# The guard in the softmax's sum, four pairs of w_out sums on VectorE, and a planner that knows GpSimd's exclusion

## The chip, the cores and the metric

The kernel runs on one core of a Trainium2 chip. The metric is the device time of one execution in microseconds, where lower is better. The core has five engines that matter here: TensorE (PE, matrix products), VectorE (DVE), ScalarE (ACT), GpSimd (POOL), and SyncE (SP), which issues the transfers.

## What is computed

Block attention feeds a feed-forward layer, all in float32. Each query sees the keys less than 16 positions away and 24 summaries of blocks of 32 keys (the maximum of the keys, the mean of the values).

```python
k_sum = k.reshape(B, H, nb, 32, D).max(axis=3)
v_sum = v.reshape(B, H, nb, 32, D).mean(axis=3)
a = np.exp(scores_all - np.max(scores_all, axis=-1, keepdims=True))
a = a / (np.sum(a, axis=-1, keepdims=True) + 1e-09)
x = np.matmul(a, np.concatenate([v, v_sum], axis=2))     # 4 batches, 8 heads, 768 x 64
h = x_as_3072_by_512 @ w_in                              # w_in 512 x 2048
out = np.square(np.maximum(h, 0.0)) @ w_out              # w_out 2048 x 512
```

## The kernel before

Every product of two float32 operands is made of three matmuls with high and low halves: a value is cast to a rounded high half, and what is left is the low half. So most results need a cast on ACT and a subtraction on DVE before PE may read them.

The program has three kinds of work on the 3072 tokens. Two *plain* units (512 tokens each) run the feed-forward layer directly: for each f of 16 blocks of d_ff, FI (line 1195) is twelve matmuls with w_in, then come Relu (RL, line 1204), square (SQ) and cast (GH, line 1206) on ACT and the subtraction GL (line 1209) on DVE, and FO (line 1219) is twelve matmuls with w_out. `rl`, which RL and SQ write and GL reads last, is a single buffer, so the RL of the next f waits for the GL of this one. Behind them, *mixed* (line 1731) and *products* (line 1514) handle the other 2048 tokens with fewer products, from sums of blocks of the weights. Those sums are made while the plain units run: `combine(p)` makes the sums for eight pairs of w_out blocks (RC: two operations of 128x512, line 1300; SC: four of 128x256, line 1315; SH, the cast, line 1318; SL, the subtraction, line 1321; then a store), and `combine_in` the half sums of w_in blocks (line 1364, 128x256; line 1379, four of 128x128; 1382 and 1385 for cast and subtraction). RC and SC of the pairs are on POOL; of the half sums, two for each of eight pairs of w_in blocks, the string HALF_SUMS_BY says pair by pair whether RC and SC are on POOL (P) or on DVE (D).

The attention is made in 48 groups of scores. For each, PE makes scores (S, line 756), DVE takes the maximum with the mask (M, line 830), ACT makes the exponentials and their sums (line 887), DVE adds 1e-9 and takes the reciprocal (R, lines 899 and 900), and the normalisation (N) is either one operation on DVE (line 906, 128x472) or four activations on ACT (line 913), as the string NORMAL_BY says. Then the square blocks are transposed (T), by PE (line 926) or by DVE with a transfer (line 955), and multiplied by the values (V, line 997).

What each engine does, and in which order, comes from a planner. The class `Plan` takes tasks (`add(name, engine, cost, emit, key, ...)`), and `order` simulates all engines in time with these costs, always starting the task with the smallest key that can start. Nothing of the order is decided on the chip: each engine works through its list, and waits where an operand is not there. Tables of numbers (VISITS for the attention's groups, COMBS and SUMS for the sums, FV_AT and others) set the keys. In the planner's model, DVE's two-input operations and POOL's exclude each other; before, this is a factor by which one stretches the other (`SLOWS`, `SLOWED`).

Of the kernel before, what the change touches and what calls it, by code (L numbers as in the profile page):

```python
# [53 lines left out]
PRODUCTS = 7  # L54
FV_AT = 60.61, 233.96
FV1_LEAD = 17.0
HALVED = 2
TURN_LATE = 0.4
COMBS = 113.9, 126.8, 141.39, 159.1, 177.9, 210.24, 223.15, 214.82
Q_LEAD = 10.72  # L60
XS_LEAD = 10
R_LEAD = 9
TR_LEAD = 16.82
VISITS = 50.65, 58.31, 70.31, 76.15, 99.76, 110.62, 136.36, 142.89, 161.01, 177.12, 203.05, 215.03, 227.83, 233.26, 248.89, 277.47, 296.02, 310.51, 324.02, 346.69, 366.69, 366.74, 394.74
X_LEAD = 5.36
SPLIT_AT = -7.62
KEPT = 105.02, 3.08
GH_LEAD = 12
# [117 lines left out]
class Plan:  # L186
# [8 lines left out]
    NARROW = ("S", "V", "VM")  # L195
    SHARED = "GL", "TA", "TB", "WJ", "WW", "SL", "SLi", "XD", "XSL", "XPL", "XW", "RCi", "SCi", "N"
# [16 lines left out]
    def order(self):  # L213
# [13 lines left out]
        events, n, pipe = [], 0, 0.0  # L227
        started, narrow, slows = [], False, 0.0
        for t in self.tasks:
            kind = t.name.rstrip("0123456789_ab")  # L230
            t.narrow = t.engine == "PE" and kind in self.NARROW
            kind = "".join(c for c in kind if not c.isdigit() and c != "_")
            t.shared = t.engine == "DVE" and kind in self.SHARED
            t.late_by = 0.25 if kind == "R" else 0.0
            t.slack = self.SLACK.get(kind, 0.0)
            t.slows = self.SLOWS.get(kind, 0.3)
            t.slowed = self.SLOWED.get(kind, 1.1) if t.engine == "POOL" else 1.0

# [15 lines left out]
        while events:  # L254
            now = events[0][0]
            while events and events[0][0] <= now + 1e-9:
                t = heapq.heappop(events)[2]
                if t is None:
                    continue
                if isinstance(t, tuple):  # L260
                    ready[t[0].engine].append(t[0])
                    continue
                for b in t.take + t.use:
                    b.left -= 1
                for x in then[t]:
                    x.wait -= 1
                    if x.wait:
                        continue
                    if x.slack:
                        n += 1  # L270
                        heapq.heappush(events, (now + x.slack, n, (x,)))
                    else:
                        ready[x.engine].append(x)
# [6 lines left out]
            for e, tasks in ready.items():  # L280
# [20 lines left out]
                started.append(t)  # L301
                cost = t.cost * t.slowed
                if e == "SP":
                    cost *= (0.40 + 0.065 * min(max(pipe - now, 0.0), 4.0)) / 0.42
                if e == "DVE" and free["POOL"] > now:
                    cost += t.late_by
                    if t.shared:
                        cost += slows * min(cost, free["POOL"] - now)
                if e == "POOL":
                    slows = t.slows  # L310
                free[e] = end = now + cost + self.SWITCH * (t.narrow and not narrow)
# [15 lines left out]
def attention_then_relu2_ffn(  # L327
# [4 lines left out]
    vS: bass.AP,  # L332
    vF: bass.AP,
    wW: bass.AP,
    out: bass.AP,
# [89 lines left out]
    MIXED_STEP = 1.54, 1.41  # L425
    X_BY = 19.41, 14.78
# [3 lines left out]
    HALF_AT = 26.97, 32.0  # L430
    MX = 0.95
# [374 lines left out]
    def softmax(g, by_pe=False):  # L806
# [15 lines left out]
        for i, t_s in enumerate(t_S[g]):  # L822
# [49 lines left out]
            def total(js=js):  # L872
                nc.vector.tensor_reduce(
                    out=nm.tile[:, NPAIR : 2 * NPAIR][:, js], in_=pr.tile[:, js, :KEYS], op=ALU.add, axis=AX.X
                )
# [9 lines left out]
        def exps(p):  # L885
            x = pr.tile[:, p, :KEYS]
            nc.scalar.activation(  # L887
                x, score_tile(g, p % parts)[:, p] if by_pe else x, AF.Exp, bias=nm.tile[:, p : p + 1],
                scale=SCALE if by_pe else -1.0, accum_out=nm.tile[:, NPAIR + p : NPAIR + p + 1],
            )  # L890
# [23 lines left out]

# [371 lines left out]
    def combine(p):  # L1286

        due = COMBS[p]
        ws = [woven[1, 2 * p + k] for k in range(2)]
        xs = [buf("t", 3, (P, 2 * DM), F32, f"c{'rs'[i]}{p}") for i in range(2)]  # L1290

        def block(c, w):
# [58 lines left out]
    def combine_in(p, k, due):  # L1351
# [43 lines left out]
        for i in range(2):  # L1395
# [3 lines left out]
            ))  # L1399
        t2 = add(f"SC{name}", engine, 1.7 * slow + 0.1, add_up, due + 0.8, t1, use=[x])  # L1400
        t3 = add(f"SH{name}", "ACT", 0.56, high, due + 2, [t2], use=[x])
# [459 lines left out]
    def groups(n):  # L1861

        nonlocal done_g
        while done_g < n:
# [122 lines left out]
```

## Time and profile before

| | |
|---|---|
| three runs | 582.85, 584.73, 585.45 us, median 584.73 |
| the profiled execution | 583.48 us |
| its span (first to last instruction) | 581.0 us |
| mean granted clock of TensorE | 0.996 |
| busy: PE, DVE, ACT, POOL | 563.0, 452.2, 373.7, 134.5 us |

The page gives each engine's busy time and the groups of instructions that took it. Other views tell who waited for whom, when each instruction started, and how busy each engine was in a stretch of time. Times in the timeline are counted from the first instruction.

### The profile page before, as it was taken

How to read it: one execution, taken by the hardware profiler on the slowest of the kernel's cores; microseconds unless marked ns; L12 is line 12 of the kernel's file. 1: busy time of each engine (PE TensorE's matmuls, PEld its weight loads, DVE VectorE, ACT ScalarE, POOL GpSimd, SP SyncE). 2: the span in 40 equal slices, each digit the busy share in tenths (PEclk: the TensorE clock that was granted, in tenths of full speed). 3: DMA queues.
4: the chain of work that ended last, by engine and by line, in shares of the span. 5: the costliest groups of instructions: out<-in, count | busy, mean ns of one | idle time of the engine just before them, and what ended most of it. 6: DMA issues, size and time to landing. Idle time of an engine off the chain costs nothing.

```text
span 581.0 us, 12047 instructions
## 1 busy us (share of the span) xinstructions
PE 563.0 (97%) x4052; PEld 460.2 (79%) x4052; DVE 452.2 (78%) x1015; ACT 373.7 (64%) x968; POOL 134.5 (23%) x193
## 2 busy tenths in 40 slices
PE   7879999999999899999999999999999999999997
PEld 6668787888887688887888888888888888888885
DVE  4899999685799997879976978869932656868864
ACT  1899899786757787768765768464634642454442
POOL 4300010167669469500043430000000000000000
PEclk9999999999999999999999999999999999999999
DMA  8899996989997999999988888866875566667672
GB/s 298 295 382 340 332 337 243 323 327 341 304 381 236 327 358 338 364 333 335 312 271 246 268 257 257 268 181 192 256 240 175 178 195 192 196 195 226 196 227 98
DMA packets 88082, 157.15 MB, mean 270 GB/s; under 512 B 9066, under 2 KB 30926, under 8 KB 88022
## 3 DMA queue, kind: packets, MB, share of 16 engines
q1 hardware_dynamic: 88022, 156.39, 82.2%
q8 instruction: 32, 0.52, 0.4%
q14 instruction: 28, 0.23, 0.1%
HBM read 111.30 MB, written 44.66 MB: 268 GB/s over the span
## 4 chain that ended last, share of the span: by engine, by line
PE 76%; DVE 9%; DMA 8%; SPq 3%; issue 2%; ACT 1%; DVEq 0%; ACTq 0%
PE o L1514 23%; PE o L1731 14%; PE h L1195 9%; PE o L1219 9%; PE sz L1731 8%; PE att L1514 4%; PE x L997 3%; DMA raw<-wW 3%; PE att L756 2%; PE sa L1731 2%; PE att L1731 2%; DMA v<-vS 1%; DMA fv_lent<-vS 1%; DMA out<-os 1%; DVE ci L1379 1%
## 5 line engine op out<-in xcount | busy, mean ns | idle before, releaser
L1496 ACT CAST gh<-g 128x512 fp32r<-128x512 f32 x112 | 69.3, 621 | 63.2 <-DVE gl L1501 30.5
L1514 PE MATMUL o<-gh,w 128*128 128x512 f32 x384 | 103.0, 390 | 0.0
L1501 DVE TENSOR_TENSOR gl<-g,gh 128x512 fp32r<-128x512 f32 x112 | 76.8, 693 | 22.9 <-ACT gh L1496 22.4
L1514 PEld LDWEIGHTS o<-gh,w 128*128 128x128 f32 x384 | 71.8, 188 | 15.0
L1195 PE MATMUL h<-xh,w 128*128 128x512 f32 x240 | 76.2, 399 | 3.9 <-ACT rl L1204 3.9
L1768 ACT ACTIVATE g<-g 128x512 f32<-128x512 f32 x60 | 37.6, 630 | 49.5 <-DVE g L1764 49.3
L887 ACT ACTIVATE p<-p,small 128x118 f32<-128x118 f32 x160 | 61.1, 387 | 1.6 <-DVE small L830 1.6
L1219 PE MATMUL o<-w,gh 128*128 128x512 f32 x240 | 61.9, 394 | 0.0
L1514 PE MATMUL o<-gl,w 128*128 128x512 f32 x192 | 59.2, 389 | 0.0
L1195 PEld LDWEIGHTS h<-xh,w 128*128 128x128 f32 x240 | 45.1, 191 | 14.2 <-ACT rl L1204 4.7
L1219 PEld LDWEIGHTS o<-w,gh 128*128 128x128 f32 x240 | 44.4, 188 | 9.7 <-issue 0.4
L1195 PE MATMUL h<-xl,w 128*128 128x512 f32 x120 | 47.2, 394 | 0.0
L1514 PEld LDWEIGHTS o<-gl,w 128*128 128x128 f32 x192 | 36.0, 188 | 7.6
L1731 PE MATMUL o<-w,w 128*128 128x512 f32 x160 | 40.6, 390 | 0.0
L769 POOL COPY kb<-kb 128x96 f32<-128x96 f32 x25 | 10.9, 435 | 107.1 <-PE att L756 36.4
L1774 POOL TENSOR_TENSOR g<-g 128x512 f32<-128x512 f32 x16 | 22.6, 1418 | 53.7 <-ACT g L1768 53.1
L1731 PEld LDWEIGHTS o<-w,w 128*128 128x128 f32 x160 | 30.0, 188 | 6.3
L1491 DVE TENSOR_TENSOR g<-g 128x512 f32<-128x512 f32 x48 | 33.9, 716 | 1.2 <-POOL g L1774 0.7
L830 DVE CUSTOM_DVE_ANT_0 p<-att,mask 128x118 f32<-128x118 f32 x152 | 32.5, 272 | 2.6 <-PE att L756 2.6
L1731 PE MATMUL sz<-xh,w 128*128 128x512 f32 x128 | 34.5, 391 | 0.0
L1219 PE MATMUL o<-w,gl 128*128 128x512 f32 x120 | 33.6, 389 | 0.0
L1764 DVE CUSTOM_DVE_ANT_0 g<-sz,g 128x512 f32<-128x512 f32 x32 | 21.9, 685 | 13.2 <-ACT g L1751 6.4
(201 smaller groups left out, 1186.7 us busy)
## 6 DMA issues: line engine op xcount, KB each, us to landing
raw<-wW SPq DMA_DIRECT2D x32, 512.0 KB
w<-scr_t SPq DMA_DIRECT2D x64, 256.0 KB
w<-scr_s SPq DMA_DIRECT2D x64, 256.0 KB
w<-scr_a SPq DMA_DIRECT2D x48, 256.0 KB
w<-scr_i SPq DMA_DIRECT2D x44, 256.0 KB
turn<-a SPq DMA_DIRECT2D x18, 512.0 KB
scr_t<-ci SPq DMA_DIRECT2D x16, 512.0 KB
v<-vS SPq DMA_DIRECT2D x34, 192.0 KB
```

The lines of the kernel that those rows point to most:

```text
L830: nc.vector.tensor_tensor_reduce(out=pr.tile[:, j, :KEYS], in0=score_at(g, 0, j), in1=mask_of(g)[0], scale=-SCALE, scalar=-NEG, op0=ALU.ad ...
L887: nc.scalar.activation(x, score_tile(g, p % parts)[:, p] if by_pe else x, AF.Exp, bias=nm.tile[:, p : p + 1], scale=SCALE if by_pe else -1 ...
L1195: nc.tensor.matmul(cut(h), lhsT=lhs.tile[:, k // 2, k % 2 * P : (k % 2 + 1) * P], rhs=rhs[:, k, c0 : c0 + n], start=(i == 0), stop=(i == 3 ...
L1219: nc.tensor.matmul(o_of(o, t).rearrange("p (h c) -> p h c", h=2), lhsT=terms[i][0].tile[:, (t - t0) * P : (t - t0 + 1) * P], rhs=terms[i][ ...
L1491: lambda x=x, ins=ins, op=op: nc.vector.tensor_tensor(out=x.tile, in0=ins[0].tile, in1=ins[1].tile, op=op),
L1496: f"GH{s}_{n}", "ACT", 0.54, lambda x=x, gh=gh: nc.scalar.copy(out=gh.tile, in_=x.tile), due - GH_LEAD, ready,
L1501: lambda x=x, gh=gh, gl=gl: nc.vector.tensor_tensor(out=gl.tile, in0=x.tile, in1=gh.tile.bitcast(F32), op=ALU.subtract),
L1514: nc.tensor.matmul(o.tile[:, d], lhsT=chunk.tile[:, w * HALF + d * P : w * HALF + (d + 1) * P], rhs=y.tile, start=begins and w == 0 and y ...
L1731: nc.tensor.matmul(o.tile, lhsT=lhs(w, k), rhs=y[k], start=begins and i == 0, stop=i == 5, skip_group_check=not begins,)
L1764: lambda: nc.vector._custom_dve(TENSOR_ADD_SAT, out=to.tile, in0=o.tile, in1=x.tile, s0=HUGE, s1=0.0), key, deps,
L1768: f"G{name}_{s}", "ACT", 0.63, lambda: nc.scalar.activation(to.tile, to.tile, AF.Square), key + 0.7, [t], use=[to]
L1774: f"{name}_{s}", engine, cost, lambda: tensor.tensor_tensor(out=to.tile, in0=a.tile, in1=b.tile, op=ALU.subtract), key, deps,
```

## The change

Six things change.

1. The tile `nm` (in the order's rows `small`) has 16 columns for a group in place of 12. The sums are in columns 8 to 11, and columns 12 to 15 hold 1e-9, set once by three memsets on POOL. R adds the two by one reduction over both (TENSOR_REDUCE, 128x4 from 128x8) where it had a TENSOR_SCALAR.
2. COMBS_BY sends RC and SC of the pairs 0, 1, 2 and 6 of w_out to DVE.
3. HALF_SUMS_BY moves which half sums are on DVE: pairs 4, 6, 7 before, 0 and 4 now.
4. NORMAL_BY has 10 groups on ACT, where it had 20.
5. The planner models exclusion exactly: it keeps the ends of the running POOL operation's pieces, and a DVE operation that needs the shared port waits for the piece that is running, and pushes the ones behind it.
6. The tables of keys are new numbers. `batch_means` and its input are new, too, but MEANS_BY = "PP" leaves them unused.

```diff
-NORMAL_BY = "DDDDDDDDDDDDAADDDDDAADDADDAAAADDADDDDAADAAAAAAAA"
-HALF_SUMS_BY = "PPPPDPDD"
+NORMAL_BY = "DDDDDDDDDDDDDDDAADDAADAADDADDADDADDDDDDDDDDADDDD"
+COMBS_BY = "DDDPPPDP"
+HALF_SUMS_BY = "DPPPDPPP"
...
-COMBS = 113.9, 126.8, 141.39, 159.1, 177.9, 210.24, 223.15, 214.82
+COMBS = 115.38, 133.05, 111.75, 161.18, 184.3, 225.3, 201.76, 232.08
...
-    SLOWS = dict(RC=1.0, TA=1.0, TB=1.0, RCi=0.75, SCi=0.4, SC=0.2)
-    SLOWED = dict(RCi=1.2, SCi=1.35, RC=1.12, SC=1.2, KC=1.4, TA=0.95, TB=0.95)
+    PORTED |= dict(SC=(4, 0.4), SCi=(4, 0.25))
+    PIECES = dict(RC=(1, 1.3), SC=(4, 0.74), RCi=(1, 0.74), SCi=(4, 0.46), KC=(1, 0.27), TA=(1, 1.3), TB=(1, 1.3), C=(0, 0.0))
...
+                if t.ported:
+                    at = now
+                    for _ in range(t.ported[0]):
+                        i = next((i for i, x in enumerate(pool) if x > at), None)
+                        if i is not None:
+                            cost += pool[i] - at
+                            at = pool[i]
+                            pool[i + 1 :] = [x + t.ported[1] for x in pool[i + 1 :]]
+                        at += t.ported[1]
...
-    SUMS = 121.7, 129.74, 148.43, 166.33, 195.88, 201.13, 197.53, 197.25, 153.98, 169.96, 168.64, 165.29, 173.06, 198.45, 180.64, 190.85
+    SUMS = 125.86, 118.08, 156.5, 165.84, 192.11, 199.75, 201.36, 194.59, 144.23, 176.48, 167.97, 152.24, 157.23, 194.46, 181.73, 203.98
...
+    def make_guard():
+        for x in small:
+            nc.gpsimd.memset(x[:, 3 * NPAIR :], 1e-9)
...
-        nm = buf("nm", 3, (P, 3 * NPAIR), F32, f"nm{g}")
+        nm = buf("nm", 3, (P, 4 * NPAIR), F32, f"nm{g}")
...
         def inverse():
-            den, rec = nm.tile[:, NPAIR : 2 * NPAIR], nm.tile[:, 2 * NPAIR : 3 * NPAIR]
-            nc.vector.tensor_scalar_add(rec, den, 1e-9)
+            rec = nm.tile[:, NPAIR : 2 * NPAIR]
+            nc.vector.tensor_reduce(
+                out=rec, in_=nm.tile[:, 2 * NPAIR :].rearrange("p (k n) -> p n k", k=2), op=ALU.add, axis=AX.X
+            )
             nc.vector.reciprocal(out=rec, in_=rec)
...
+        by_pool = COMBS_BY[p] == "P"
+        engine, tensor = ("POOL", nc.gpsimd) if by_pool else ("DVE", nc.vector)
...
-            nc.gpsimd.tensor_tensor(
+            tensor.tensor_tensor(
                 out=halves(k, 0), in0=ws[k][0].tile.bitcast(F32), in1=ws[k][1].tile.bitcast(F32), op=ALU.add
             )
```

Three places show how the order moves. The first is DVE's list where the second unit begins (`gl_0` is the GL of its first f; `cr` and `cs` are the tiles of a w_out pair, `p` the exponentials, `a` their transposes). Before:

```order
L1385 TENSOR_TENSOR ci_1_1906<-ci_1_1906 128x4x128
L899 TENSOR_SCALAR small_88<-small_88 128x4
L900 RECIPROCAL small_88<-small_88 128x4
L899 TENSOR_SCALAR small_72<-small_72 128x4
L900 RECIPROCAL small_72<-small_72 128x4
L906 TENSOR_TENSOR p_83<-p_83,small_72 128x4x118
L955 STREAM_TRANSPOSE a_2046<-p_82 128x4x128
L955 STREAM_TRANSPOSE a_2046<-p_83 128x4x128
L1321 TENSOR_TENSOR cr_1955<-cr_1955 128x2x256
L1321 TENSOR_TENSOR cs_1956<-cs_1956 128x2x256
L1209 TENSOR_TENSOR gl_0_2095<-rl_0_2044,gh_0_2054 128x512
```

Now (line 965 is R's reduction, 1277 is GL, 1391 is SL, 1370 is RC and 1385 SC):

```order
L968 RECIPROCAL small_72<-small_72 128x4
L974 TENSOR_TENSOR p_83<-p_83,small_72 128x4x118
L1023 STREAM_TRANSPOSE a_2046<-p_82 128x4x128
L1391 TENSOR_TENSOR cr_1957<-cr_1957 128x2x256
L1023 STREAM_TRANSPOSE a_2046<-p_83 128x4x128
L1391 TENSOR_TENSOR cs_1958<-cs_1958 128x2x256
L1370 TENSOR_TENSOR cr_2090<-w_2_916 128x2x256
L1370 TENSOR_TENSOR cs_2091<-w_849 128x2x256
L1277 TENSOR_TENSOR gl_0_2097<-rl_0_2050,gh_0_2055 128x512
L1385 TENSOR_TENSOR cs_2091<-cr_2090,cs_2091 128x256
L1385 TENSOR_TENSOR cr_2090<-cs_2091,cr_2090 128x256
L1385 TENSOR_TENSOR cr_2090<-cr_2090 128x256
```

The subtractions of the pair before stand there as they did; the two additions (line 1370) and the four others (line 1385) of a pair are new in the row, on both sides of `gl_0`.

The second place is DVE's list from the GL of the seventh f of that unit (`gl_6`) to that of the eighth (`gl_7`); `ci` are the tiles of half sums. Before:

```order
L955 STREAM_TRANSPOSE a_2609<-p_82 128x4x128
L899 TENSOR_SCALAR small_72<-small_72 128x4
L900 RECIPROCAL small_72<-small_72 128x4
L1385 TENSOR_TENSOR ci_0_2446<-ci_0_2446 128x4x128
L1385 TENSOR_TENSOR ci_1_2428<-ci_1_2428 128x4x128
L1379 TENSOR_TENSOR ci_0_2566<-ci_0_2566 128x128 x4
L955 STREAM_TRANSPOSE a_2609<-p_83 128x4x128
L1364 TENSOR_TENSOR ci_0_2657<-w_1684 128x2x128
L1364 TENSOR_TENSOR ci_0_2657<-w_1665 128x2x128
L1385 TENSOR_TENSOR ci_0_2566<-ci_0_2566 128x4x128
L1379 TENSOR_TENSOR ci_0_2657<-ci_0_2657 128x128 x4
L1209 TENSOR_TENSOR gl_7_2672<-rl_7_2614,gh_7_2659 128x512
```

Now, with the row ahead of `gl_6` (lines 1434 and 1449 make a half sum, 1455 is its subtraction):

```order
L1434 TENSOR_TENSOR ci_1_2578<-w_1137 128x2x128
L1277 TENSOR_TENSOR gl_6_2585<-rl_6_2504,gh_6_2512 128x512
L1023 STREAM_TRANSPOSE a_2602<-p_82 128x4x128
L965 TENSOR_REDUCE small_72<-small_72 128x4
L968 RECIPROCAL small_72<-small_72 128x4
L1434 TENSOR_TENSOR ci_1_2578<-w_1176 128x2x128
L974 TENSOR_TENSOR p_83<-p_83,small_72 128x4x118
L1455 TENSOR_TENSOR ci_1_2406<-ci_1_2406 128x4x128
L1023 STREAM_TRANSPOSE a_2602<-p_83 128x4x128
L1455 TENSOR_TENSOR ci_0_2501<-ci_0_2501 128x4x128
L1449 TENSOR_TENSOR ci_1_2578<-ci_1_2578 128x128 x4
L1277 TENSOR_TENSOR gl_7_2667<-rl_7_2621,gh_7_2641 128x512
```

Two times four operations of line 1379 and two of 1364 stood between these two GLs; now four and one of their counterparts stand there, and a normalisation (line 974).

The third place is PE's list around f = 6 of the first unit (`h_6` is FI, `o` are FO's, `t` a transposition). Before:

```order
L1219 MATMUL o_67<-w_828,gh_3_1015 128x512 x4
L1219 MATMUL o_66<-w_828,gh_3_1015 128x512 x4
L1219 MATMUL o_67<-w_828,gl_3_1022 128x512 x2
L1219 MATMUL o_66<-w_828,gl_3_1022 128x512 x2
L926 MATMUL t_1083<-ident,p_83 128x128 x4
L1195 MATMUL h_6_1091<-xh,w_975 128x512 x2
L1195 MATMUL h_6_1091<-xl,w_975 128x512
```

Now (line 1263 is FI, 1287 is FO, 994 the transposition):

```order
L1287 MATMUL o_67<-w_849,gl_3_1039 128x512 x2
L1287 MATMUL o_66<-w_849,gl_3_1039 128x512 x2
L994 MATMUL t_1085<-ident,p_83 128x128 x4
L1287 MATMUL o_67<-w_893,gh_4_1060 128x512 x4
L1287 MATMUL o_66<-w_893,gh_4_1060 128x512 x4
L1287 MATMUL o_67<-w_893,gl_4_1080 128x512 x2
L1287 MATMUL o_66<-w_893,gl_4_1080 128x512 x2
L1263 MATMUL h_6_1118<-xh,w_982 128x512 x2
L1263 MATMUL h_6_1118<-xl,w_982 128x512
```

FI of f = 6 stood directly behind the transposition; now FO of f = 4 stands between the two.

## Rows read from the trace of the kernel before

**Rows 1.** The page's busy shares of the engines, in us of the span.

```profile
PE 563.0 (97%) x4052; PEld 460.2 (79%) x4052; DVE 452.2 (78%) x1015; ACT 373.7 (64%) x968; POOL 134.5 (23%) x193
```

**Rows 2.** Waits on PE: line waited for, us in total, times, longest.

```profile
PE h L1195 <- ACT rl L1204: 3.9, 3, 2.7
...
PE o L1731 <- DVE g L1764: 0.3, 1, 0.3
```

**Rows 3.** Timeline of PE at two places: start, us, instruction, idle before.

```profile
69.79 0.73 PE L1195 MATMUL h<-xh,w 128*128 128x512 f32 x2 [0.81 <-ACT rl L1204]
...
72.65 1.98 PE L1219 MATMUL o<-w,gh 128*128 128x512 f32 x8
...
201.23 1.22 PE L1195 MATMUL h<-xh,w 128*128 128x512 f32 x2 [2.72 <-ACT rl L1204]
...
205.62 1.08 PE L1219 MATMUL o<-w,gh 128*128 128x512 f32 x4
```

**Rows 4.** Busy us of PE, PEld, DVE, ACT, POOL, then clock, DMA, GB/s.

```profile
100.00:146.40 46.40, 46.40 (x372) 37.98 (x371) 32.25 (x90) 35.74 (x99) 22.10 (x27) 1.00 0.92 329
146.40:202.00 55.60, 52.51 (x446) 42.55 (x445) 50.69 (x127) 39.42 (x112) 38.35 (x51) 0.99 0.90 308
201.20:204.60 3.40, 3.37 (x8) 2.69 (x9) 3.40 (x20) 3.36 (x12) 2.47 (x4) 0.51 1.07 390
```

**Rows 5.** Waits on ACT of line 1204.

```profile
ACT rl L1204 <- DVE gl L1209: 13.8, 10, 3.9
```

**Rows 6.** Timeline of ACT before the stall ends.

```profile
195.08 1.25 ACT L913 ACTIVATE p<-p,small 128x118 f32<-128x118 f32 x4 [0.38 <-DVE small L900]
...
199.92 0.62 ACT L1382 CAST ci<-ci 128x512 fp32r<-128x512 f32 x1 [1.00 <-DVE ci L1379]
...
200.58 0.60 ACT L1204 ACTIVATE rl<-h 128x512 f32<-128x512 f32 x1
```

**Rows 7.** Timeline of DVE, three of line 1209.

```profile
183.69 0.85 DVE L1209 TENSOR_TENSOR gl<-rl,gh 128x512 fp32r<-128x512 f32 x1
...
193.05 0.95 DVE L1209 TENSOR_TENSOR gl<-rl,gh 128x512 fp32r<-128x512 f32 x1
...
199.81 0.68 DVE L1209 TENSOR_TENSOR gl<-rl,gh 128x512 fp32r<-128x512 f32 x1
```

**Rows 8.** DVE's groups of half sums from 146.4 to 202 us.

```profile
L1379 DVE TENSOR_TENSOR ci<-ci 128x128 f32<-128x128 f32 x16 | 6.8, 463 | 0.2
...
L1364 DVE TENSOR_TENSOR ci<-w 128x256 f32<-128x256 f32 x8 | 5.7, 740 | 0.5 <-DMA out<-os 0.5
```

**Rows 9.** DVE's groups over the whole span, shapes apart.

```profile
L1209 DVE TENSOR_TENSOR gl<-rl,gh 128x512 fp32r<-128x512 f32 x30 | 25.2, 842 | 6.2 <-ACT gh L1206 6.2
...
L899 DVE TENSOR_SCALAR small<-small 128x4 f32<-128x4 f32 x48 | 12.2, 254 | 5.5 <-ACT p L887 4.5 <-ACT qvpa_lent L887 1.0
...
L900 DVE RECIPROCAL small<-small 128x4 f32<-128x4 f32 x48 | 8.5, 178 | 1.6
...
L906 DVE TENSOR_TENSOR qvpa_lent<-qvpa_lent,small 128x472 f32<-128x472 f32 x8 | 5.1, 641 | 0.1
...
L873 DVE TENSOR_REDUCE small<-qvpa_lent 128x2 f32<-128x236 f32 x2 | 0.8, 394 | 0.5 <-ACT qvpa_lent L870 0.5
```

**Rows 10.** POOL's groups of sums over the whole span.

```profile
L1379 POOL TENSOR_TENSOR ci<-ci 128x128 f32<-128x128 f32 x40 | 24.9, 643 | 1.2
...
L1364 POOL TENSOR_TENSOR ci<-w 128x256 f32<-128x256 f32 x20 | 16.1, 822 | 18.5 <-DMA scr_t<-ci 7.2 <-DMA scr_s<-cr 6.2 <-DVE ci L1379 5.1
...
L1300 POOL TENSOR_TENSOR cs<-w 128x512 f32<-128x512 f32 x8 | 13.0, 1622 | 17.0 <-DVE w L1145 14.8 <-PE h L1195 2.3
...
L1315 POOL TENSOR_TENSOR cs<-cr,cs 128x256 f32<-128x256 f32 x8 | 7.5, 942 | 0.4
```

**Rows 11.** One GL on DVE, and the matmuls on PE that read it.

```profile
164.85 1.13 DVE L1209 TENSOR_TENSOR gl<-rl,gh 128x512 fp32r<-128x512 f32 x1
...
178.85 1.07 PE L1219 MATMUL o<-w,gl 128*128 128x512 f32 x4
```

More of the change, by code (lines that the diff above doesn't have):

```diff
@@ L232, in order @@
             kind = "".join(c for c in kind if not c.isdigit() and c != "_")
-            t.shared = t.engine == "DVE" and kind in self.SHARED
-            t.late_by = 0.25 if kind == "R" else 0.0
+            t.ported = self.PORTED.get(kind) if t.engine == "DVE" else None
+            if t.ported and not t.ported[1]:
+                t.ported = 1, t.cost - 0.13
+            t.pieces = self.PIECES.get(kind, (1, t.cost)) if t.engine == "POOL" else None
             t.slack = self.SLACK.get(kind, 0.0)
-            t.slows = self.SLOWS.get(kind, 0.3)
-            t.slowed = self.SLOWED.get(kind, 1.1) if t.engine == "POOL" else 1.0
         def can(t):
@@ L258, in order @@
                 if t is None:
+                    continue
+                if not isinstance(t, tuple) and t.engine == "POOL" and t.end + self.HOP > now + 1e-9:
+                    n += 1
+                    heapq.heappush(events, (t.end + self.HOP, n, t))
                     continue
@@ L301, in order @@
                 started.append(t)
-                cost = t.cost * t.slowed
+                cost = t.cost
                 if e == "SP":
                     cost *= (0.40 + 0.065 * min(max(pipe - now, 0.0), 4.0)) / 0.42
[L305 to L310, printed above, removed]
+                if t.ported:
[7 more added lines that the diff above has]
+                        at += t.ported[1]
+                    port = at
+                    if pool and pool[-1] > free["POOL"]:
+                        free["POOL"] = running.end = pool[-1]
+                        n += 1
+                        heapq.heappush(events, (pool[-1], n + 0.5, None))
+                if t.pieces:
+                    k, d = t.pieces
+                    at = max(now, port) if k else now
+                    pool, running = [at + d * (i + 1) for i in range(k)], t
+                    cost = pool[-1] + 0.03 - now if k else cost
                 free[e] = end = now + cost + self.SWITCH * (t.narrow and not narrow)
@@ L594, in attention_then_relu2_ffn, with batch_means, load, sums @@
     t_means = add("means", "POOL", 1.0, make_means, -88)
+    def make_guard():
+        for x in small:
+            nc.gpsimd.memset(x[:, 3 * NPAIR :], 1e-9)
+    t_guard = add("guard", "POOL", 0.3, make_guard, -87)
+    NQT = DM // P
+    ROWS = BLOCK // 4
+    def batch_means(b):
+        key = FV_AT[b - 2]
+        xs = [buf("t", 3, (P, 2 * DM), F32, f"fv{b}_{i}") for i in range(BLOCK // ROWS)]
+        n = NB * NQT
+        def load(i):
+            nc.sync.dma_start(out=xs[i].tile[:n], in_=vB[b - 2, :, i])
+        def sums(i):
+            return xs[0].tile[:n, i * P : (i + 1) * P]
+        def add_up(i):
+            nc.vector.tensor_reduce(
+                out=sums(i), in_=xs[i].tile[:n].rearrange("p (r c) -> p c r", c=P), axis=AX.X, op=ALU.add
+            )
+        def mean():
+            k = len(xs)
+            nc.vector.tensor_reduce(
+                out=sums(k), in_=xs[0].tile[:n, : k * P].rearrange("p (k c) -> p c k", c=P), axis=AX.X, op=ALU.add
+            )
+            nc.vector.tensor_scalar_mul(out=sums(k), in0=sums(k), scalar1=1.0 / BLOCK)
+        t = None
+        for i, x in enumerate(xs):
+            tl = add(
+                f"FV{b}_{i}", "SP", 0.42, lambda i=i: load(i), key + FV_GAP * i, take=[x], size=4 * n * 2 * DM * RUN4,
+                begin=key - 2 + FV_GAP * i, keeps=True,
+            )
+            t = add(f"VR{b}_{i}", "DVE", 1.15, lambda i=i: add_up(i), key + FV_GAP * i + 3, [tl, t], use=[xs[0], x] if i else [x])
+        t = add(f"VR{b}", "DVE", 0.85, mean, key + FV_GAP * 3 + 4, [t], use=xs[:1])
+        t_VS[b] = [add(
+            f"VD{b}", "SP", 0.42, lambda: nc.sync.dma_start(out=scr_v[b].rearrange("n (q c) -> (n q) c", c=P), in_=sums(len(xs))),
+            t.key + 1.5, [t], use=xs[:1], size=4 * NB * DM,
+        )]
     def batch_v(b):
@@ L873, in total @@
                 nc.vector.tensor_reduce(
-                    out=nm.tile[:, NPAIR : 2 * NPAIR][:, js], in_=pr.tile[:, js, :KEYS], op=ALU.add, axis=AX.X
+                    out=nm.tile[:, 2 * NPAIR : 3 * NPAIR][:, js], in_=pr.tile[:, js, :KEYS], op=ALU.add, axis=AX.X
                 )
@@ L1399, in combine_in @@
             ))
-        t2 = add(f"SC{name}", engine, 1.7 * slow + 0.1, add_up, due + 0.8, t1, use=[x])
+        t2 = add(f"SC{name}", engine, 1.8 if by_pool else 1.2, add_up, due + 0.8, t1, use=[x])
         t3 = add(f"SH{name}", "ACT", 0.56, high, due + 2, [t2], use=[x])
```

48 lines of the change are left out of this document (28 added, 20 removed).

## The prediction

> **What bounds the kernel now.** I read the page first, for the busy shares: TensorE is busy 97% of the span, VectorE 78% [rows 1]. PE does the same instructions before and after the change, so only its gaps can be won or lost, and gaps that PE makes itself (start-up apart) are few. The second view is who waited for whom on PE: after the start-up, the matmuls of line 1195 (FI, the w_in products of one f) waited three times for the Relu of line 1204, 3.9 us in all and 2.7 at the longest, and one product of the mixed stage waited 0.3 us for VectorE [rows 2]. The third is PE's timeline. The longest wait is 2.72 us ahead of 201.23, and the twelve matmuls behind it take 4.39 us to the next group's start (205.62); a like group at 69.79 to 72.65 takes 2.86 us [rows 3]. So the stall has a second cost of 4.39 - 2.86 = 1.53 us: in the 3.4 us behind it the granted clock is 0.51, which is the lower of TensorE's two levels, 1.2 GHz, where the stretch of 100 to 146.4 us shows 1.00 [rows 4]. PE was idle for 2.72 us just before. Together that one place costs 4.25 us. At 69.79 the wait is 0.81 us [rows 3], and the third must be 3.9 - 2.7 - 0.8 = 0.4 us.
>
> Why the Relu is late: on ScalarE, line 1204 waits ten times for VectorE's line 1209, 13.8 us in all [rows 5]; `rl` is a single buffer, and GL (line 1209) is its last reader. Ahead of the late Relu at 200.58 stands the cast of line 1382, which idled 1.00 us for VectorE's line 1379 [rows 6], the quarter sums of a w_in half sum. On VectorE three GLs lie at 183.69, 193.05 and 199.81, that is 9.4 and 6.8 us apart [rows 7], while PE needs about 5.7 us for each f (FI and FO, twice the 2.86). VectorE, then, is behind in this stretch: from 146.4 to 202 us it is busy 50.69 of 55.6 us (91%); from 100 to 146.4 only 32.25 of 46.4, so 14.15 us are free there, while GpSimd works 22.10 us in the first and 38.35 us in the second [rows 4].
>
> **The change, part by part.** *Half sums.* From 146.4 to 202 VectorE does 16 operations of line 1379 and 8 of 1364, four half sums, in 6.8 + 5.7 = 12.5 us [rows 8]. In the new order only two of them stand between the GLs of f 0 and 7 of the second unit; two others (pair 0) stand before the first unit's last GLs. An operation of 128x256 costs about 0.41 us (estimate: the reduction that reads 236 columns takes 0.394 [rows 9]), one of 128x128 less, some 0.27 (estimate: about two thirds of it). A half sum free of GpSimd is then 2 x 0.41 + 4 x 0.27 = 1.9 us; the measured 12.5 / 4 = 3.1 is the upper bound.
>
> *Four w_out pairs.* A pair on VectorE is two operations of 128x512 at 0.68 (the GL at 199.81 [rows 7]) and four of 128x256 at 0.41: 3.0 us, 12 us for four. On GpSimd it takes 2 x 1.62 + 4 x 0.94 = 7.0 us [rows 10]; 28 us leave that engine, two more half sums come (2 x 0.82 + 4 x 0.64 = 4.2 us each, at the means of [rows 10]). The order puts pairs 2 and 0 and the first two operations of pair 1 ahead of the second unit's first GL.
>
> *Normalisations.* Ten more are on VectorE. One is 0.64 us when GpSimd is quiet [rows 9]; ScalarE loses four activations each, which start over 1.25 us for four [rows 6]. Most lie behind 300 us, where PE shows no wait for it; two (g = 12, 13) fall around 105 us.
>
> *The guard.* 48 additions of 1e-9 to 128x4 take 0.254 us in the mean, the reciprocal of the same shape 0.178 [rows 9]. A reduction of 128x8 to 128x4 is not in the trace; from below nothing at all bounds it, from above the reduction of 2 x 118 to 2 columns, 0.394 [rows 9]. I take 0.18, as its size is nearest to the reciprocal's. That is -3.6 us of VectorE over the run, with bounds of -12 and +6.7; six of these lie in the stretch of the stall, so -0.4 us there (bounds -1.5 to +0.8). The three memsets lie in GpSimd's start-up, ahead of work that waits for scores.
>
> One rule speaks against this edit. The Trainium skill (VectorE: DVE Perf Modes, Rules for kernel authors) says that a tensor_reduce on a hot path is the slowest operation of that engine and should be restructured away. By the trace 236 columns take 0.394 us, so at eight columns the rule has little to act on; by the rule's worst reading, the 0.394, the sum would be 0.8 us worse at the stall.
>
> *The ledger of the two stretches.* From 100 to 146.4, VectorE gains 3.0 + 3.0 + 1.4 (pairs) + 3.8 (half sums) + 1.3 (normalisations) = 12.5 us, against 14.15 free: it fits with little left, and what spills is met by slack. The GL at 164.85 is read by PE only at 178.85 [rows 11], so 13 us of lateness cost nothing there. From 146.4 to 202, it loses 12.5 and gains 1.6 (the rest of pair 1) + 3.8 (two half sums): -7.1 us. The Relu of 200.58 has to come 2.72 us earlier, that of the 0.4 us stall 0.4: 7.1 covers both, unless more than 4.4 us spill over from the first stretch.
>
> *What else is saved.* GL takes 0.842 us in the mean and 0.68 when nothing is on GpSimd [rows 7, 9]: 30 x 0.16 = 4.8 us of waiting, part of which goes as GpSimd has 28 - 8.4 = 20 us less to do. I count it as reserve.
>
> *PE's order.* In the new order the group that waited 0.81 us stands behind another FO group of some 2.86 us, whose operands are older; that covers the wait. Without that cover the 0.81 comes back.
>
> *Planner.* The exact exclusion costs nothing by itself; it acts through these orders.
>
> **Sum.** -4.25 (stall and clock) - 0.8 - 0.4 = -5.45; the 0.3 us at VectorE's other wait stays. Every retimed table brings small waits somewhere: I add two of the sizes seen, 0.4 and 0.8, so -4.25 in all. The profiled execution took 583.48 us (span 581.0 and 2.48 around it): 579.2. The median of the runs shown is 584.73, 1.25 higher; by it the sum is 580.5. I say 579.5.
>
> **Rivals.** A measurement of this kernel can tell about 0.5% (2.9 us) from no change: faster is below 581.8, slower above 587.6.
>
> 1. *The backlog moves.* VectorE gains 12.5 us in a stretch with 14.15 free. If its waits for data (which made part of the free time) stay, over 10 us of GL lateness arise by the second unit's first f, and one stall of the same kind, with its clock, comes there: -5.45 + 4.25 + 1 = about 583.5. For it: the pairs stand directly ahead of GL in the row. Against: 13 us of slack and a GpSimd that is idle there, so shorter operations. 0.18.
>
> 2. *Half the relief.* 4 to 5 us spill over; the wait of 2.72 shrinks to about 1, and its clock loss falls away or not: 580.5 to 582.5. 0.12, most of it faster.
>
> 3. *Slower: GpSimd's sums come late.* ScalarE takes the casts of the sums (lines 1318, 1382) in order ahead of Relu; [rows 6] show one that idled 1.00 us. By the tables GpSimd's first sum moves from 113.9 to 152.24 us, and by the order twelve half sums of 4.2 us and pairs 3 and 4 of 7.0 us follow, 64 us of work without a break. If a sum is over 5 us behind its place, the cast stalls ScalarE, then Relu, then PE; two such places, each with its clock, cost 8.5, and if half of the 5.45 is still won, the time is 583.5 - 2.7 + 8.5 = 589.3. For it: GpSimd had 38.35 of 55.6 us of work there [rows 4]. Against: it loses the pairs. 0.10.
>
> 4. *Nothing for PE.* The reduction comes out at its upper bound and each stretch of VectorE stays as late as it was: 583.5. 0.04. The rule of the Trainium skill named above would act this way.
>
> The forecast itself, with its range of 576.5 to 581.8, has 0.56.
>
> **How the numbers follow.** Faster: 0.56 + 0.10 of the second rival = 0.66. Same: 0.18 + 0.02 + 0.04 = 0.24. Slower: 0.10. The range must leave out no more than 0.2: its low end takes in a start-up gain that I could not price, 575.5; its high end takes the first rival with the noise of the runs, 585.5, and leaves out the third.
>
> **What would show it.** Right: no PE gap over 1 us behind 60 us for line 1204's counterpart; a granted clock of 1.00 near 200 us; GLs of the second unit at most 6 us apart from f 5 to 7; the guard's reduction at about 0.18 us, not longer while GpSimd runs. Wrong: a PE gap with a half clock at 145 to 165 us (the first rival), or ScalarE waiting for GpSimd's sums at 180 to 240 us (the third), or VectorE busy over 95% in both stretches.

## The result and the profile after

The changed kernel takes 579.37 us in the median (578.37 to 581.89) against 584.73 for the kernel before in the same measurement; the ratio is 0.9912, 95% interval 0.9886 to 0.9937. The profiled execution took 579.34 us, with a span of 577.5. The prediction was 579.5.

The page gives the busy shares:

```profile
PE 563.2 (98%) x4052; PEld 460.9 (80%) x4052; DVE 456.4 (79%) x1037; ACT 365.0 (63%) x928; POOL 119.5 (21%) x184
```

PE's busy time is what it was [rows 1], so between these two executions the 3.5 us of the span are waits. VectorE's busy time does not fall: 456.4 us in place of 452.2. GpSimd loses 15 us.

Who waited for whom on PE (us in total, times, longest):

```profile
PE t L994 <- DVE qvpa_lent L974: 2.6, 2, 1.9
...
PE h L1263 <- DVE xl L1133: 1.9, 1, 1.9
...
PE h L1263 <- ACT rl L1272: 0.2, 1, 0.2
```

The wait for Relu, 3.9 us before [rows 2], is 0.2 (line 1272). A wait of 1.9 us for XL is new (line 1133, the low half of the attention's output; the tile that it reads shares two buffers with those into which FI writes, so FI waits for it). Another wait is nearly gone, at the start: at 41 us, the first matmuls of `h_0b` (FI of f = 0 for half of the first unit's tokens) waited for the cast XH, the high half of the attention's output. Before, and now:

```profile
PE h_0b L1195 <- ACT xh L1062: 1.7, 1, 1.7
```

```profile
PE h_0b L1263 <- ACT xh L1130: 0.2, 1, 0.2
```

The timeline of VectorE, at the GLs that answer to [rows 7]:

```profile
186.73 0.94 DVE L1277 TENSOR_TENSOR gl<-rl,gh 128x512 fp32r<-128x512 f32 x1
...
193.26 3.06 DVE L1449 TENSOR_TENSOR ci<-ci 128x128 f32<-128x128 f32 x4
196.25 1.23 DVE L1277 TENSOR_TENSOR gl<-rl,gh 128x512 fp32r<-128x512 f32 x1
```

The last two GLs ahead of the stall's place lie at 186.73 and 196.25, still 9.5 us apart, with a half sum's four operations (3.06 us) between them. But they are 6.3 and 3.6 us earlier than they were. ScalarE's timeline, as in [rows 6]:

```profile
194.15 0.62 ACT L1452 CAST ci<-ci 128x512 fp32r<-128x512 f32 x1 [2.26 <-POOL ci L1449]
196.36 0.62 ACT L1452 CAST ci<-ci 128x512 fp32r<-128x512 f32 x1 [1.58 <-DVE ci L1449]
197.56 0.60 ACT L1272 ACTIVATE rl<-h 128x512 f32<-128x512 f32 x1 [0.59 <-DVE gl L1277]
```

Two casts still wait for their sums there, but the Relu comes at 197.56, where it came at 200.58, and the FI that waited till 201.23 now starts at 198.76 without a wait. PE's last work ahead of this FI, before:

```profile
197.36 1.15 PE L997 MATMUL x<-a,v 118*64 118x64 f32 x32
```

and the FI now, with what follows it:

```profile
198.76 0.73 PE L1263 MATMUL h<-xh,w 128*128 128x512 f32 x2
...
201.61 1.98 PE L1287 MATMUL o<-w,gh 128*128 128x512 f32 x8
```

PE has done the same matmuls up to this FI in both kernels (as many of each kind). Before, they end at 198.51, now at 198.76: up to there nothing is won in this pair of executions. From there to the end of the FI's twelve matmuls it took 7.1 us before (to 205.62 [rows 3]) and takes 2.9 now (to 201.61): 4.3 us are won at the stall.

Busy time by stretch (PE, PEld, VectorE, ScalarE, GpSimd, then the clock, DMA share, GB/s):

```profile
28.00:36.00 8.00, 6.14 (x82) 5.04 (x83) 7.43 (x22) 7.07 (x25) 1.03 (x3) 0.79 1.02 400
100.00:146.40 46.40, 44.54 (x362) 36.17 (x361) 35.83 (x112) 35.51 (x101) 0.91 (x2) 1.00 0.81 277
146.40:202.00 55.60, 55.39 (x461) 45.31 (x461) 52.62 (x137) 42.62 (x124) 40.72 (x55) 1.00 0.97 339
```

Against [rows 4], VectorE is busier in both stretches: 35.83 and 52.62 us, where it was 32.25 and 50.69. And the clock: the stretch of 0.51 at 201 us is gone, but 28 to 36 us show 0.79. So each of these two executions has one stretch of the lower clock; the mean clock of many executions, in the table below, differs.

### The profile page after: what moved, and what is told of

It reads as the page before. It is cut to its first block, busy times and chain, and to the rows that moved or that the text cites. A ratio compares the mean times of both kernels' runs of the same rounds, so it can differ in the third digit from the quotient of the medians.

```text
span 577.5 us, 12008 instructions
## 1 busy us (share of the span) xinstructions
PE 563.2 (98%) x4052; PEld 460.9 (80%) x4052; DVE 456.4 (79%) x1037; ACT 365.0 (63%) x928; POOL 119.5 (21%) x184
## 4 chain that ended last, share of the span: by engine, by line
PE 80%; DMA 9%; DVE 5%; SPq 3%; ACT 2%; issue 1%; DVEq 0%; ACTq 0%
PE o L1584 23%; PE o L1801 13%; PE o L1287 11%; PE h L1263 11%; PE sz L1801 7%; PE att L1584 4%; PE x L1065 3%; DMA raw<-wW 3%; PE sa L1801 3%; PE att L822 3%; PE att L1801 2%; DMA q<-qW 2%; DMA turn<-a 1%; DMA scr_v<-fv_w 1%; DMA fv_lent<-vS 1%
```

## Experiments

All are compared with runs of the kernel before on the same chip. Two ways of editing were used. In the first, the planner orders anew; in the second, each engine's list stays as it was, and only the engine that executes an operation, or the place of a few named operations, is changed. The second takes one thing at a time. The last column is the mean of the granted clocks of the run's executions; for the kernel before it is 0.994 (70 executions, on three chips), for the changed kernel 0.998 (five).

| run | median us | ratio to before, 95% interval | mean clock |
|---|---|---|---|
| guard_only | 584.62 | 0.9993 (0.9970 to 1.0015) | 0.994 |
| guard_old | 579.34 | 0.9923 (0.9886 to 0.9960) | 0.998 |
| pairs_on_pool | 578.90 | 0.9893 (0.9875 to 0.9911) | 0.999 |
| normals_swapped | 580.73 | 0.9917 (0.9887 to 0.9947) | 0.998 |
| halves_swapped | 584.10 | 0.9978 (0.9960 to 0.9996) | 0.997 |
| before_halves | 585.62 | 1.0022 (1.0002 to 1.0043) | 0.993 |
| before_pairs | 585.73 | 1.0016 (0.9991 to 1.0042) | 0.994 |
| before_both | 586.06 | 1.0022 (1.0003 to 1.0041) | 0.993 |
| combs_pool | 590.76 | 1.0106 (1.0066 to 1.0147) | 0.989 |
| pair2_late | 587.76 | 1.0050 (1.0033 to 1.0067) | 0.990 |
| pair2_behind | 579.09 | 0.9908 (0.9883 to 0.9933) | 0.999 |
| half4_behind | 579.36 | 0.9916 (0.9883 to 0.9948) | 0.999 |

### The guard, alone and taken back

guard_only puts the guard of the change into the kernel before (cut here to R; the columns and the memsets move with it):

```diff
...
-            nc.vector.tensor_scalar_add(rec, den, 1e-9)
+            nc.vector.tensor_reduce(
+                out=rec, in_=nm.tile[:, 2 * NPAIR :].rearrange("p (k n) -> p n k", k=2), op=ALU.add, axis=AX.X
+            )
...
```

> The kernel before with the guard alone: 1e-9 in a column, R as a reduction; every engine's order as it was. Theory M (the sums' engines and places made the gain): R falls from 0.254 to about 0.15 us in the mean, 5 us of VectorE over the run but only six R's (1.4 us) in the stretch from 146 to 202 us; the 2.72 us stall shrinks to 1.3 to 2.7 us and the time is 582 to 584.5. Rival G (the waits of the guard's addition for GpSimd were the backlog): the stall and its half clock go, 579 to 580.5.

guard_old puts the addition back into the changed kernel:

```diff
-            nc.vector.tensor_reduce(
-                out=rec, in_=nm.tile[:, 2 * NPAIR :].rearrange("p (k n) -> p n k", k=2), op=ALU.add, axis=AX.X
-            )
+            nc.vector.tensor_scalar_add(rec, nm.tile[:, 2 * NPAIR : 3 * NPAIR], 1e-9)
```

> The changed kernel with the old addition of 1e-9 in R; every engine's order as in the changed kernel. Theory M: R lengthens where GpSimd runs, to 0.2 to 0.26 us in the mean, covered by VectorE's slack: 579 to 580.5, no stall over 1 us behind 150 us. Rival G: a stall of 2 us or more with the lower clock returns near 200 us: 583 or more.

VectorE's group of R's addition in the changed kernel, and under it that of guard_old:

```profile
L965 DVE TENSOR_REDUCE small<-small 128x4 f32<-128x8 f32 x48 | 7.3, 153 | 4.4 <-ACT p L953 4.2
```

```profile
L965 DVE TENSOR_SCALAR small<-small 128x4 f32<-128x4 f32 x48 | 13.3, 276 | 4.4 <-ACT p L953 4.2
```

The reduction takes 0.153 us, the addition 0.276: 5.9 us of VectorE over the run. Neither run's time can be told from its counterpart without that edit, so rival G is out. Theory M holds with small misses: guard_only's median is 0.1 us above its range, and in guard_old the addition took longer than its 0.2 to 0.26 us, while PE waited for Relu again, three times up to 1.0 us:

```profile
PE h L1261 <- ACT rl L1270: 2.4, 3, 1.0
```

PE's timeline in guard_only at the stall:

```profile
200.13 0.73 PE L1204 MATMUL h<-xh,w 128*128 128x512 f32 x2 [2.52 <-ACT rl L1213]
...
202.99 1.98 PE L1228 MATMUL o<-w,gh 128*128 128x512 f32 x8
```

The wait is 2.52 us, in the range of theory M, and the twelve matmuls behind it take 2.86 us (200.13 to 202.99): no lower clock followed there. This execution has its lower clock elsewhere, behind the wait for XH (1.7 us, up to 40.11):

```profile
42.00:46.00 4.00, 4.00 (x18) 3.58 (x18) 3.97 (x13) 4.00 (x15) 0.00 (x0) 0.57 1.03 400
```

### The engine of the pairs and of the normalisations

pairs_on_pool leaves every list of the changed kernel, but GpSimd executes the additions of pairs 0, 1, 2 and 6 at their places:

```diff
-        engine, tensor = ("POOL", nc.gpsimd) if by_pool else ("DVE", nc.vector)
+        engine, tensor = "POOL" if by_pool else "DVE", nc.gpsimd
```

> The changed kernel with its order kept, except that GpSimd executes the additions of pairs 0, 1, 2 and 6 at the same places. Theory M (VectorE's share of the sums matters): pairs take 6 to 7 us in place of 3, their casts on ScalarE come later, VectorE waits for GpSimd again between 120 and 150 us; PE waits of 2 us or more near 127 to 165: 581 to 585. Rival T (the new order alone made the gain): the 127 us wait falls, as VectorE has 12 us less to do, and the time is 577 to 579.5.

578.90 us: theory M fell, Rival T held, and the wait at 127 us does not appear in its profile. In this order it makes no difference that can be measured which engine adds the four pairs.

normals_swapped takes each normalisation's function from the old string and leaves its place:

```diff
+        by = normal_by_act if "DDDDDDDDDDDDAADDDDDAADDADDAAAADDADDDDAADAAAAAAAA"[g] == "A" else normal
...
-            t_n = add(f"N{g}", "DVE", 0.56, normal, due - 10, [t_r], use=[pr, nm])
+            t_n = add(f"N{g}", "DVE", 0.56, by, due - 10, [t_r], use=[pr, nm])
```

> The changed kernel with its order kept, except that each normalisation is on the engine of before (10 more on ScalarE). Theory M (they lie where nothing waits): 578.5 to 580. Rival A (ScalarE was too full for them): a PE wait for Relu or for the cast of line 1566 of 1 us or more, 580.5 to 583.

The ratio, 0.9917, is that of the changed kernel within both intervals; the median lies in rival A's range by 0.2 us, which these runs can't tell from the changed kernel's. Rival A's wait did come in the profiled execution, the slowest of the six (583.32 us):

```profile
PE h L1264 <- ACT rl L1273: 2.2, 2, 1.3
```

So these runs do not rule rival A out; if it costs something, it is too little for them to show.

### The engine of the half sums

halves_swapped does the same with the half sums: every list of the changed kernel, but pairs 4, 6 and 7 on VectorE and 0 on GpSimd.

```diff
+        tensor = nc.gpsimd if "PPPPDPDD"[p] == "P" else nc.vector
```

> The changed kernel with its order kept, except that the half sums are on the engines of before (pairs 4, 6 and 7 on VectorE, 0 on GpSimd). Theory M: VectorE gets four more half sums between 165 and 215 us (8 us and more with waits), GL falls behind and a PE wait for Relu of 2 to 4 us with the lower clock returns between 165 and 205: 582 to 586. Rival T: the half sums fit at their new places on either engine: 579 to 580.5.

584.10 us: theory M's range, and the only single part whose return takes the gain away. ScalarE's timeline shows how:

```profile
198.88 0.63 ACT L1453 CAST ci<-ci 128x512 fp32r<-128x512 f32 x1 [2.18 <-DVE ci L1450]
201.96 0.62 ACT L1453 CAST ci<-ci 128x512 fp32r<-128x512 f32 x1 [2.45 <-DVE ci L1450]
202.62 0.60 ACT L1272 ACTIVATE rl<-h 128x512 f32<-128x512 f32 x1
```

Two casts of half sums (line 1453 here) wait 2.18 and 2.45 us for VectorE's additions. Relu stands behind them in ScalarE's list, and PE behind Relu:

```profile
203.28 0.73 PE L1263 MATMUL h<-xh,w 128*128 128x512 f32 x2 [1.33 <-ACT rl L1272]
```

This wait is smaller than theory M had it, and the clock stays up behind it. At 172 us PE waits for a GL, and ahead of that GL VectorE adds half sums that came late themselves:

```profile
169.06 2.37 DVE L1435 TENSOR_TENSOR ci<-w 128x256 f32<-128x256 f32 x4 [1.39 <-DMA scr_s<-cr]
171.34 0.68 DVE L1277 TENSOR_TENSOR gl<-rl,gh 128x512 fp32r<-128x512 f32 x1
```

```profile
172.08 1.20 PE L1287 MATMUL o<-w,gl 128*128 128x512 f32 x4 [1.57 <-DVE gl L1277]
```

These two waits are 2.9 us of PE. The rest came from elsewhere: in this execution, the second slowest of the twelve (586.26 us), PE also waited 1.7 us for a copy of the output, 1.5 for transfers, and 2.4 for the XL at 127 us, where the changed kernel waits 1.9, with the lower clock from 127 to 130 us. That these follow from the swap was not shown.

### The new engines in the old order

before_halves, before_pairs and before_both leave every list of the kernel before, and let the half sums, the pairs, or both be executed by the engines of the change:

```diff
+        tensor = nc.gpsimd if "DDDPPPDP"[p] == "P" else nc.vector
...
-            nc.gpsimd.tensor_tensor(
+            tensor.tensor_tensor(
...
+        tensor = nc.gpsimd if "DPPPDPPP"[p] == "P" else nc.vector
```

The first string is that of the pairs, the last that of the half sums.

> The kernel before with its order kept, except that the half sums are on the engines of the change (pairs 0 and 4 on VectorE, 6 and 7 on GpSimd). Theory H (the half sums on VectorE between 146 and 202 us were the backlog): the 2.72 us stall ahead of 201 falls below 1 us, 579 to 582. Rival O (they can only go to GpSimd in the new order, since GpSimd is already 69% busy there): ScalarE's casts wait for GpSimd's sums, PE waits for Relu of 2 us or more between 185 and 225: 584 to 590.

> The kernel before with its order kept, except that VectorE does the additions of pairs 0, 1, 2 and 6. Theory H: the half sums stay on VectorE, so the stall near 200 us stays; pairs 0 to 2 lie in its free time, and pair 6 (3.0 us) falls in the stretch behind 202 us: 583 to 587. Rival S (GpSimd's operations make VectorE wait, and with the pairs gone from it those waits go): the stall falls below 1 us, 579.5 to 582.

> The kernel before with its order kept, except that pairs and half sums are both on the engines of the change. Theory H: with the pairs off GpSimd the half sums fit there; the stall near 200 us falls below 1 us, 579 to 582. Rival O (the new order is needed): PE waits of 2 us or more between 120 and 225 us, 583 to 588.

None is faster than before. before_pairs came out as theory H has it (the stall stays, 2.7 us), and rival S fell. For before_halves and before_both theory H fell: the stall is 2.0 us, where it had less than 1, and a wait of 1.4 us for Relu at 217 us is new in both. VectorE's timeline in before_both:

```profile
192.38 0.94 DVE L1209 TENSOR_TENSOR gl<-rl,gh 128x512 fp32r<-128x512 f32 x1
...
197.84 0.95 DVE L1209 TENSOR_TENSOR gl<-rl,gh 128x512 fp32r<-128x512 f32 x1
```

The last GL ahead of the stall is at 197.84, where it was at 199.81 [rows 7]. But ScalarE:

```profile
200.00 0.62 ACT L1385 CAST ci<-ci 128x512 fp32r<-128x512 f32 x1 [1.76 <-POOL ci L1382]
200.53 0.59 ACT L1204 ACTIVATE rl<-h 128x512 f32<-128x512 f32 x1
```

The cast ahead of Relu (line 1385 here, 1382 before) now waits for GpSimd's addition, 1.76 us, and ends at 200.62, where it ended at 200.54 when it waited for VectorE [rows 6]. PE waits 2.02 us in place of 2.72. Rival O of before_halves and before_both is borne out: in the order of before, the new engines gain nothing.

### New plans from the same tables

combs_pool and pair2_late let the planner order anew with one entry changed:

```diff
-COMBS_BY = "DDDPPPDP"
+COMBS_BY = "PPPPPPPP"
```

> The changed kernel with all eight w_out pairs on GpSimd; the planner orders anew with the same tables. Theory M: GpSimd starts its sums 40 us earlier, VectorE's two-input operations wait for it again, GL grows from 0.79 to 0.84 us in the mean, and a PE wait of 1 to 3 us returns behind 150 us, while the 1.9 us wait at 127 us goes: 580 to 584. Rival T (the new places in the tables made the gain, whichever engine adds): 577.5 to 579.5.

```diff
-COMBS = 115.38, 133.05, 111.75, ...
+COMBS = 115.38, 133.05, 121.75, ...
```

> The changed kernel with the due time of w_out pair 2 at 121.75 in place of 111.75, so that its four additions of 128x256 stand behind the subtraction XL that PE waited for at 127.28. Theory P (pair 2 stood in VectorE's way): that wait of 1.86 us falls to about 0.2: 577 to 578.5. Rival W (the late weights made the burst, and the rest of it is long enough): the wait stays at 1.2 us or more: 579 to 580.

Both are slower, and both for a reason that no theory had named: the new plans put the first scores of the last batch some products earlier, ahead of the keys' maximum (line 586), which waits for the loads of the keys. PE's timeline in combs_pool at the wait, and the stretch behind it:

```profile
259.19 0.66 PE L822 MATMUL att<-kb,q 64*64 64x118 f32 x4 [5.80 <-DVE kb L586]
```

```profile
256.00:268.00 12.00, 7.59 (x69) 5.33 (x70) 11.63 (x29) 5.84 (x15) 1.03 (x3) 0.50 0.83 291
```

5.80 us of waiting, and twelve microseconds at the lower clock, which begin within the wait. So combs_pool says nothing of the pairs' engine; pairs_on_pool, which kept the order, does. In pair2_late the wait at 127 us fell from 1.86 to under 0.5, which theory P had as its sign, and the other one cost more. All four ranges foretold for these two runs were missed.

### The wait at 127 us

The chain of work in the changed kernel ahead of that wait, and what stood on VectorE:

```profile
108.13 8.76 DMA raw<-wW
...
127.28 0.73 PE h L1263 x2
```

```profile
120.46 0.69 DVE L1370 TENSOR_TENSOR cr<-w 128x512 f32<-128x512 f32 x1
...
123.48 0.42 DVE L1385 TENSOR_TENSOR cs<-cr,cs 128x256 f32<-128x256 f32 x1
...
126.54 0.69 DVE L1133 TENSOR_TENSOR xl<-x,xh 128x512 fp32r<-128x512 f32 x1
```

A weight's transfer, issued at 107.75 behind an earlier one, takes 8.76 us; behind it everything comes at once, and pair 2's six additions (lines 1370 and 1385, 120.46 to 124.94 with others) stand ahead of the XL at 126.54. pair2_behind keeps the order, but puts the six behind XL, and the cast of their first sum later on ScalarE:

```diff
...
+        for name, place in (("RC2_0", "E18_3"), ("RC2_1", "E18_3"), ("SC2", "E18_3"), ("SH2_0", "SH2_1")):
+            t = tasks[name]
+            started.remove(t)
+            started.insert(started.index(tasks[place]), t)
...
```

> The changed kernel with its order kept, except that the six additions of w_out pair 2 stand behind the subtraction XL on VectorE, and the cast of their first sum behind the exponentials on ScalarE. Theory P (pair 2, 3.0 us, stood ahead of the XL that PE waited for at 127.28): XL ends 2.5 to 3 us earlier, the wait of 1.86 us falls below 0.5, and no other PE wait grows by more than 0.5: 577 to 578.2. Rival W (late weights set that place): the wait stays over 1.2 us, 579 to 580.

In that run FI starts at 124.33 without a wait: theory P is right about that place. Its waits on PE:

```profile
PE o L1801 <- ACT os L1324: 2.3, 1, 2.3
...
PE h L1263 <- DVE xl L1133: 0.9, 1, 0.9
```

But the time is the changed kernel's, 579.09 in the median, in the range of rival W although W's mechanism fell: in the profiled execution (581.92 us) the next XL holds PE 0.9 us at 144, and a copy of the output 2.3 us at 255. That the first of these follows from the edit is plausible (the six additions push what follows them); that the second does wasn't shown.

half4_behind starts from pairs_on_pool, and moves a half sum of pair 4, with its cast, its subtraction and its store, behind two GLs that it held up at 164 to 170 us:

```diff
...
+        for name, place in (("RCi4_0_0", "RL1_3"), ("RCi4_0_1", "RL1_3"), ("SCi4_0", "SLi4_0"), ("SHi4_0", "XH21"), ("SLi4_0", "SLi6_0"), ("WSi4_0", "WSi1_0")):
...
```

> The changed kernel with the four pairs on GpSimd at their places, and on VectorE the half sum of pair 4 behind the GLs of f = 2 and 3 of the second unit, which it held up at 164 to 170 us. Theory Q (an addition that waits for a buffer or for GpSimd holds the GL behind it): the PE wait of 1.2 us for Relu at 170 us falls below 0.4, 576.5 to 578.5. Rival: the GL's lateness has another cause, or the next small wait takes its place: 578.5 to 580.

```profile
PE h L1263 <- ACT rl L1272: 1.5, 4, 1.0
PE o L1801 <- DMA w<-scr_t: 1.2, 1, 1.2
PE h L1263 <- DVE xl L1133: 1.0, 1, 1.0
```

The wait at 170 us fell from 1.2 in pairs_on_pool to 0.15, as theory Q has it, and waits of about 1 us for XL, for Relu elsewhere (1.5 in four) and for a transfer of sums took its place: the rival. No version here beats the changed kernel by more than can be measured.

## Why the prediction came out right, and where it was wrong

*The stall.* "-4.25 (stall and clock) - 0.8 - 0.4": the waits for Relu went as foretold, 3.9 to 0.2 us. At the stall the step holds in its details: the Relu had to come 2.72 us earlier and came 3.0 earlier (200.58 to 197.56), and 4.3 us were won there, where 4.25 were foretold.

*The clock* in that term, 1.53 us, went at that place, but the two profiled executions cannot show what it is worth, since the changed kernel's has a stretch of the lower clock at 30 us instead. The mean clocks can: 0.994 for the kernel before and 0.993 to 0.994 for the four runs in its order, 0.998 for the changed kernel and 0.997 to 0.999 for the six runs that keep its order. One minus the mean clock, times the span, is 3.6 us for the kernel before and 1.2 for the changed one (an estimate from these clocks), so nearly half of the gain of 5.4 us is clock, and it comes with the order. Not all of it lies at the stall: of the five profiles in the order of before, four have the lower clock there, and four have it at 41 to 46 us, behind the wait for XH.

*What the sum did not have* is the start. The prediction names a gain there that it could not price and puts it into the range alone. PE's waits up to 45 us add up to 9.6 us before and 6.7 now. The wait for XH is most of the difference: it is 1.7 us in all five profiles in the order of before, whichever engines add, and 0.2 in all nine with the new tables, so it is the order's.

*The new small waits*, 1.2 us in the sum, came out as 2.9 behind 60 us: one of 1.9, with its mechanism in rival 1 (pairs ahead of work for PE) at a place that it had not named, 127 us, and three of 0.3 to 0.4. The gain at the start paid for these and for the lower clock at 30 us. So the prediction came out right by its main step, the stall; that the sum lies within 0.2 us of the measured median is luck, as terms that it did not have cancel.

*A sign that failed.* The GLs were to be at most 6 us apart, from 5.7 us of PE for each f. They are 9.5 apart and nothing waits, as PE also does scores and products with the values between two f: its FIs at 191.18 and 198.76 are 7.6 us apart without a wait.

*The ledger failed.* It had VectorE at +12.5 us from 100 to 146.4, and -7.1 from 146.4 to 202; measured are +3.6 and +1.9. The first is smaller since part of the work listed lies past the edge (pair 1's first additions are at 148.3 and 148.9 us), and probably since GpSimd does next to nothing there (0.91 us busy, before 22.10): pairs_on_pool, where GpSimd is busy 15.47 us, has VectorE at 35.33 though the pairs are off it. The second has the wrong sign. VectorE's groups from 146.4 to 202 us:

```profile
L1455 DVE TENSOR_TENSOR ci<-ci 128x512 fp32r<-128x512 f32 x8 | 8.9, 1135 | 0.0
L1277 DVE TENSOR_TENSOR gl<-rl,gh 128x512 fp32r<-128x512 f32 x9 | 8.6, 951 | 0.0
...
L1449 DVE TENSOR_TENSOR ci<-ci 128x128 f32<-128x128 f32 x8 | 6.1, 797 | 0.1
...
L1434 DVE TENSOR_TENSOR ci<-w 128x256 f32<-128x256 f32 x4 | 1.9, 487 | 0.7 <-DMA scr_s<-cr 0.7
```

The half sums' additions fell from 12.5 us [rows 8] to 6.1 + 1.9 = 8.0, not to 3.8, as the 128x128 ones take 0.797 us in the mean while GpSimd runs, where the prediction put 0.27. GL takes 0.951 here, and the eight subtractions of the sums 8.9 us, where they took 5.7. The reserve, "4.8 us of waiting, part of which goes", was 1.6 us over the run, where GL fell from 0.842 to 0.787.

So the ledger, by which VectorE has 7.1 us less to do in that stretch, is not what made the gain: VectorE does as much there as before, and what counts is what stands ahead of the GL and the casts for which Relu waits. The runs show in its place that the order made the gain, together with the half sums' engines for which it was made: in the new order the half sums' old engines give 4.7 us back (584.10 against 579.37), while guard, pairs and normalisations can each be undone with no measured loss (they were not undone together); in the old order none of the new engines brings anything. Which of the retimed numbers does it, and what part the planner's exact exclusion has in finding them, was not tried.

*The guard* was priced at 0.18 us and takes 0.153. The rule of the Trainium skill (VectorE: DVE Perf Modes, Rules for kernel authors), that a tensor_reduce is the slowest operation of that engine, does not bear on eight columns here: the reciprocal of four takes 0.178, and the addition that it replaced 0.276. Rival 4 is out.

*A pair* on VectorE was priced at 3.0 us and takes 3.4 (13.5 us for four). *PE's order* at 69.79: "that covers the wait" was right, with 0.4 us left for a transposition there. *Rival 3's* mechanism, a cast on ScalarE that waits for GpSimd's sum ahead of Relu, was given 0.10; before_both shows it, and halves_swapped shows the same with VectorE's sums. The changed kernel has such waits too (2.26 and 1.58 us), early enough to cost PE nothing.

## What to carry to other kernels

Where every engine works through a fixed list, an operation's new engine and its place are one change: test them apart by keeping the lists and swapping only the executing engine, and then the other way round. Look past the engine that is busiest to the list in which the waited-for operation stands: here Relu stood behind casts, and the casts waited for whichever engine made the sums. And a wait that is taken away at one place is worth only what the next one leaves; two edits here removed 1 to 2 us at a place and won nothing. Last, compare the clock over many executions: one profile of each kernel hid that nearly half of the gain was clock.

## What the runs showed of the hardware

A wait of PE is sometimes followed by the lower clock (1.2 GHz) and sometimes not. The kernel before waits 2.72 us at the stall and 3.4 us at 0.51 follow, but guard_only waits 2.52 us at the same place of the same order and the clock stays at 1.00. The wait for XH at 41 us is 1.7 us in all five profiles of that order, and the lower clock follows it in four. The changed kernel has it at 28 to 36 us, near a wait of 1.87, and not behind one of 1.86 at 127. In combs_pool, with a wait of 5.80 us, it was 0.50 for 12 us. So one execution does not tell what a wait costs in clock: compare the mean clocks of many, as above, where the two orders lie at 0.994 and 0.998.

VectorE's reduction of 128x8 takes 0.116 to 0.176 us in its 48 places in the changed kernel, 0.153 in the mean, whether GpSimd runs or not. The addition of a constant that it replaces takes 0.164 in the median and up to 1.258 in the same order, 0.276 in the mean.
